# Loading tiles 0-1 from SyncE's DMA queue instead of ScalarE's, in a pruned matrix product

## The chip, the cores and the metric

The kernel runs on one core of one Trainium2 chip. The metric is the device time of one launch in microseconds (us); lower is better. Every number below comes from runs of the kernel before and from one profiled execution of it.

## The reference

The weights `w` (1024 x 1024, bf16) are pruned in groups of four along the rows: of each four values in a column, the two largest in magnitude stay and the others become zero. The pruned weights are then multiplied with the activations, and a bias is added.

```
B, S, D = 16, 512, 1024
wg   = w.reshape(D // 4, 4, D)
mag  = abs(wg)
thr  = second largest of mag along axis 1
wp   = (wg * (mag >= thr)).reshape(D, D)
out  = einsum("bsd,df->bsf", x, wp) + b
```

All is in bf16: 8192 tokens by 1024 inputs, 1024 outputs.

## The kernel before

The 8192 tokens are 64 tiles of 128. TensorE multiplies each tile with the pruned weights, eight blocks of 128 inputs and two halves of 512 outputs a tile; VectorE adds the bias as it moves the result out of PSUM; ScalarE's queue stores it. From tile 8 on a tile's transposed activations come from a transposing DMA (`xlead` for tiles 8 to 11, `xb` for the rest, 4 or 8 tiles at a time).

The first 30 us are different, because the weights must be pruned first. The weights are loaded in pieces, and each piece is pruned as it comes: magnitudes (`abs`), the larger and smaller of pairs (`hi`, `lo`), the threshold (`t1`, `t2`, `thr`), the mask and the product (`mask`, `mult`), nearly all on VectorE. Pieces 0 to 3 are 256 columns each of the upper half of the inputs, pieces 4 and 5 are 512 columns each of the lower half. In the first pieces a partition holds the four rows of one group; for later tiles the finished weights are spread to the natural order (`wp_nat`) by DMAs that SyncE (SP) issues, tokens `W0.0`, `W0.1` and so on.

Meanwhile TensorE works on tiles 0 to 7 with the pieces that are ready. Their activations are loaded by plain DMAs, `load_x`, and transposed on TensorE against an identity (line 189, token `T`); ScalarE copies the transposed tile from PSUM to SBUF (line 194, token `C`); then come the products of that tile with a piece (line 215, token `M7.0x` for tile 7, piece 0, first two of its four blocks). There are two PSUM banks for transposes, so a third transpose waits for the first copy. Before any of that TensorE runs products of constant ones into a bank that nobody reads (line 133), 22 in all, 8 of them under the token `F8`.

The order of each engine's work is written out by hand as a string of tokens, and `seq` chains the instructions of each engine in that order. TensorE starts `F8 T7a T5a T6a M7.0x M5.0x M6.0x T1a T0a M7.0y ...`; ScalarE starts `C7a C5a C6a C1a C0a`; SP's list is `W0.0 X0 X1 W0.1 Y1 ...`, where `X` and `Y` are transposing loads.

The loads at the very start are issued on two queues, SP's and ScalarE's (ACT's), by `issue(eng, ...)` at line 98: `load_w(g, c0, c1, ma, mb, eng)` loads rows `ma` to `mb` of the groups of half `g`, columns `c0` to `c1`; `load_x(ta, tb, eng)` loads the upper half of the inputs of tiles `ta` to `tb - 1`. In the order of lines 110 to 124 this makes, with the starts of the issues in the trace:

- SP: piece 0, row 0 (0.73) and row 2 (1.18); tiles 5-6 (1.64); piece 1 (2.11); tile 4 (2.99); tiles 2-3 (3.47); pieces 2 and 3 (3.95); piece 4 (4.55); the bias (5.23); piece 5 (6.10).
- ACT: piece 0, row 1 (0.74) and row 3 (1.17); tile 7 (1.66); tiles 0-1 (2.14); then the activation `spark` at line 116, whose table load starts at 2.63.

Of the kernel before, what the change touches and what calls it, by code (L numbers as in the profile page):

```python
# [10 lines left out]
def kernel(  # L11
# [64 lines left out]
    def act(i):  # L76
        return seq("act", i)
# [13 lines left out]
    def tokens(dram, t):  # L91
        a, b_ = next(s for s in GROUPS if s[0] <= t < s[1])
        return dram[a * P:b_ * P].rearrange("(p t) k -> p t k", p=P), t - a
    bias_sb = const.tile([P, Dout], bf16)

    def issue(eng, out_, in_):
        q = nc.sync if eng == "sp" else nc.scalar
        return seq(eng, q.dma_start(out_, in_))  # L98

    def load_w(g, c0, c1, ma=0, mb=4, eng="sp"):  # L100
        issue(eng, w_sb[:, g, ma:mb, c0:c1], wv[:, g, ma:mb, c0:c1])

    def load_x(ta, tb, eng="sp"):
        xs = const.tile([P, tb - ta, HK], bf16, name=f"x_{ta}")
        xv, n = tokens(xf, ta)
        issue(eng, xs[:], xv[:, n:n + tb - ta, :HK])
        for t in range(ta, tb):
            x_sb[t] = xs[:, t - ta, :]
# [3 lines left out]
    load_w(0, 0, 256, 2, 3)  # L112
    load_w(0, 0, 256, 3, 4, "act")
    load_x(7, 8, "act")
    load_x(0, 2, "act")
    act(nc.scalar.activation(spark[:], nc.const_aps.tensor(1.0, [P, 1], bf16), Act.Abs))
    load_x(5, 7)
    load_w(0, 256, 512)
    load_x(4, 5)
    load_x(2, 4)  # L120
# [368 lines left out]
```

## Time and profile before

| | |
|---|---|
| Median of 5 runs | 233.81 us (233.54 to 234.2) |
| The profiled execution's own time | 233.81 us |
| Its span, first to last instruction | 232.0 us |
| TensorE matmul (PE), busy | 226.7 us, 98% |
| VectorE (DVE), busy | 108.0 us, 47% |
| ScalarE (ACT), busy | 13.3 us, 6% |
| GpSimd (POOL), busy | 17.6 us, 8% |
| Granted TensorE clock | 1.0 throughout |

PE is the matmul side of TensorE and PEld its weight loads, which overlap the products. SPq and ACTq are the DMA issues of SyncE and ScalarE. A line such as `5.26 0.43 PE tp L189 x4` gives start and length in us, the engine, what it writes, the kernel's line and the number of instructions; `[0.44 <-DMA ...]` is idle time just before it and what ended it. In a table by stretches, each engine's busy time stands with its instruction count, then the granted clock, the share of the 16 DMA engines' time that was busy, and what they moved in GB/s.

### The profile page before, as it was taken

How to read it: one execution, taken by the hardware profiler on the slowest of the kernel's cores; microseconds unless marked ns; L12 is line 12 of the kernel's file. 1: busy time of each engine (PE TensorE's matmuls, PEld its weight loads, DVE VectorE, ACT ScalarE, POOL GpSimd, SP SyncE). 2: the span in 40 equal slices, each digit the busy share in tenths (PEclk: the TensorE clock that was granted, in tenths of full speed). 3: DMA queues.
4: the chain of work that ended last, by engine and by line, in shares of the span. 5: the costliest groups of instructions: out<-in, count | busy, mean ns of one | idle time of the engine just before them, and what ended most of it. 6: DMA issues, size and time to landing. Idle time of an engine off the chain costs nothing.

```text
span 232.0 us, 2828 instructions
## 1 busy us (share of the span) xinstructions
PE 226.7 (98%) x1139; PEld 112.2 (48%) x1158; DVE 108.0 (47%) x184; ACT 13.3 (6%) x27; POOL 17.6 (8%) x15
## 2 busy tenths in 40 slices
PE   7999999999999999999999999999999999999995
PEld 4787444544444444444444444444444444444443
DVE  4899867754234334334334324424424424423434
ACT  2665100000000000000000000000000000000000
POOL 1000199700000000000000000000000000000000
PEclk9999999999999999999999999999999999999999
DMA  6999999997299221992239821695228932122122
GB/s 186 354 215 216 222 182 252 345 206 271 95 217 280 90 93 50 233 278 75 90 96 262 230 93 48 165 285 147 84 90 197 271 120 76 62 90 82 58 89 90
DMA packets 78268, 38.19 MB, mean 165 GB/s; under 512 B 63664, under 2 KB 70576, under 8 KB 78256
## 3 DMA queue, kind: packets, MB, share of 16 engines
q1 hardware_dynamic: 67328, 20.61, 42.1%
q10 hardware_dynamic: 10928, 17.40, 20.8%
q8 instruction: 9, 0.15, 0.3%
q14 instruction: 3, 0.02, 0.1%
HBM read 3.41 MB, written 16.78 MB: 87 GB/s over the span
## 4 chain that ended last, share of the span: by engine, by line
PE 96%; DMA 2%; issue 1%; ACTq 0%; ACT 0%; DVE 0%
PE ps L238 87%; PE ps L215 6%; DMA x<-in_x_dram 2%; PE tp L238 1%; PE tp L189 1%; ACTq L98 0%; ACT xt L194 0%; DVE o L398 0%
## 5 line engine op out<-in xcount | busy, mean ns | idle before, releaser
L238 PE MATMUL ps<-wp_nat,xb 128*128 128x512 bf16 (+2 forms) x832 | 178.9, 375 | 0.8
L238 PEld LDWEIGHTS <-xb 128*128 128x128 bf16 x848 | 82.4, 98 | 97.5
L398 DVE TENSOR_TENSOR o<-ps,bias_sb 128x512 bf16<-128x512 f32 (+1 forms) x112 | 71.6, 677 | 114.3 <-PE ps L238 112.0
L394 POOL TENSOR_TENSOR st<-st,bias_sb 128x1024 f32<-128x1024 f32 x8 | 16.7, 2132 | 0.0
L215 PE MATMUL ps<-wp,xt 128*128 128x256 bf16 x128 | 15.1, 273 | 0.0
L238 PE MATMUL ps<-wp_nat,xlow 128*128 128x512 bf16 x62 | 14.0, 379 | 0.1
L215 PEld LDWEIGHTS <-xt 128*128 128x128 bf16 x128 | 12.2, 98 | 2.1 <-ACT xt L194 0.5
L400 DVE TENSOR_TENSOR o<-ps,st 128x512 bf16<-128x512 f32 x16 | 11.1, 692 | 2.8 <-PE ps L238 2.1
L238 PE MATMUL ps<-wp_nat,xlead 128*128 128x512 bf16 x47 | 11.1, 379 | 0.1
L238 PEld LDWEIGHTS <-xlow 128*128 128x128 bf16 x64 | 7.2, 112 | 6.7
L238 PEld LDWEIGHTS <-xlead 128*128 128x128 bf16 x64 | 6.2, 97 | 7.1
L255 ACT COPY st<-ps 128x512 f32<-128x512 f32 x16 | 8.5, 598 | 6.6 <-PE ps L215 4.3
L154 DVE TENSOR_TENSOR mag<-mag,hi 128x512 bf16<-128x512 bf16 (+2 forms) x8 | 5.4, 690 | 0.2
L154 DVE TENSOR_TENSOR wp<-w_sb,mag 128x512 bf16<-128x512 bf16 (+2 forms) x8 | 5.4, 690 | 0.2
L133 PE MATMUL ps<-const-bfloat16-1.0 128*128 128x128 bf16 (+1 forms) x22 | 3.9, 356 | 0.8 <-PEq L473 0.8
L164 DVE TENSOR_SCALAR mag<-w_sb 128x512 uint16<-128x512 uint16 (+2 forms) x6 | 2.7, 466 | 3.4 <-DMA w_sb<-in_w_dram 3.4
L238 PE MATMUL tp<-wp_nat,xlead 128*128 128x512 bf16 x16 | 4.1, 379 | 0.0
L189 PE MATMUL tp<-ident,x 128*128 128x128 bf16 x32 | 2.8, 220 | 0.8 <-DMA x<-in_x_dram 0.6
L133 PEld LDWEIGHTS <-const-bfloat16-1.0 128*128 128x128 bf16 x22 | 2.1, 125 | 2.4 <-issue 2.4
L154 DVE TENSOR_TENSOR hi<-mag 128x512 bf16<-128x512 bf16 (+2 forms) x7 | 3.2, 459 | 0.1
L154 DVE TENSOR_TENSOR lo<-mag 128x512 bf16<-128x512 bf16 (+2 forms) x7 | 3.2, 458 | 0.0
L194 ACT COPY xt<-tp 128x256 f32<-128x256 f32 x8 | 2.7, 380 | 3.6 <-PE tp L189 3.6
(15 smaller groups left out, 13.3 us busy)
## 6 DMA issues: line engine op xcount, KB each, us to landing
out_dram<-o ACTq DMA_DIRECT2D x59, 256.0 KB, 2.4
wp_nat<-wp SPq DMA_DIRECT2D x14, 128.0 KB, 3.5
w_sb<-in_w_dram SPq DMA_DIRECT2D x3, 512.0 KB, 6.9
out_dram<-o ACTq DMA_DIRECT2D x8, 128.0 KB, 1.7
x<-in_x_dram SPq DMA_DIRECT2D x2, 256.0 KB, 4.4
w_sb<-in_w_dram SPq DMA_DIRECT2D x1, 256.0 KB, 5.3
x<-in_x_dram ACTq DMA_DIRECT2D x1, 256.0 KB, 4.6
bias_sb<-in_b_dram SPq DMA_DIRECT2D x1, 256.0 KB, 6.9
```

The lines of the kernel that those rows point to most:

```text
L133: pe(nc.tensor.matmul(warm_ps[:, :rep * P], lhsT=nc.const_aps.tensor(1.0, [P, P], bf16), rhs=nc.const_aps.tensor(1.0, [P, rep * P], bf16), ...
L154: dve(nc.vector.tensor_tensor(out, a, b_, op=op))
L164: dve(nc.vector.tensor_single_scalar(self.mag[:, ms, :].bitcast(u16), self.w[:, ms, :].bitcast(u16), 0x7FFF, op=Alu.bitwise_and))
L189: pe(nc.tensor.transpose(tp[:, m, :], xg[:, m, :], ident[:]))
L194: act(nc.scalar.copy(xt[:].bitcast(fp32), xpk[t].bitcast(fp32)))
L215: pe(nc.tensor.matmul(ps[:, c0 + d:c1 + d], lhsT=xpk[t][:, m, :], rhs=wp[:, g, m, c0:c1], start=(new and m == ms.start), stop=(left[(q, n) ...
L238: pe(nc.tensor.matmul(ps, lhsT=xt[:, kt - koff, :], rhs=wp_nat[:, kt, c0:c1], start=(kt == first), stop=(kt == last)))
L255: act(nc.scalar.copy(st[:, n % 2, :, :].rearrange("p t c -> p (t c)"), ps_open.pop((q, n))[:]))
L394: pool(nc.gpsimd.tensor_tensor(st[:], st[:], bias[:, :, None, :].to_broadcast([P, 2, 2, CW]), op=Alu.add))
L398: dve(nc.vector.tensor_tensor(o[:, c0:c1], ps, bias_sb[:, c0:c1], op=Alu.add))
L400: dve(nc.vector.tensor_tensor(o[:, c0:c1].rearrange("p (n c) -> p n c", n=2), ps.rearrange("p (n c) -> p n c", n=2), add, op=Alu.add))
```

## The change

The load of tiles 0-1 is issued from SP's queue instead of ACT's. In the program it moves behind the load of tiles 5-6, so that on SP's queue it stands between tiles 5-6 and piece 1 of the weights. On ACT's queue the activation `spark` follows directly on the load of tile 7. Nothing else differs: the same bytes, the same tiles, the same order of work on TensorE, VectorE and ScalarE afterwards.

```
     load_w(0, 0, 256, 3, 4, "act")
     load_x(7, 8, "act")
-    load_x(0, 2, "act")
     act(nc.scalar.activation(spark[:], nc.const_aps.tensor(1.0, [P, 1], bf16), Act.Abs))
     load_x(5, 7)
+    load_x(0, 2)
     load_w(0, 256, 512)
     load_x(4, 5)
     load_x(2, 4)
```

More of the change, by code (lines that the diff above doesn't have):

```diff
@@ L114 @@
     load_x(7, 8, "act")
-    load_x(0, 2, "act")
     act(nc.scalar.activation(spark[:], nc.const_aps.tensor(1.0, [P, 1], bf16), Act.Abs))
     load_x(5, 7)
+    load_x(0, 2)
     load_w(0, 256, 512)
```

## The prediction, as put on record before the result

> **What bounds the kernel now.** I read first the page's chain, for the engine that sets the end; then the same chain in order of time, for the load on it; then the DMA issues of the first 2.5 us one by one; last the timelines, for the first user of each load that the change touches. The shares of the chain by engine:
>
> ```profile
> PE 96%; DMA 2%; issue 1%; ACTq 0%; ACT 0%; DVE 0%
> ```
>
> TensorE sets the end. A load can cost only if TensorE waits for what comes of it. The chain's start, columns start, length, what:
>
> ```profile
> 1.66 3.56 DMA x<-in_x_dram
> 5.21 0.05 issue
> 5.26 0.43 PE tp L189 x4
> 5.69 0.02 issue
> 5.71 0.38 ACT xt L194
> 6.09 0.04 issue
> 6.13 0.38 PE tp L189 x4
> ```
>
> The load on the chain is tile 7's, third on ACT's queue. It lands at 5.21; the last filler product ends at 4.70, so TensorE stands 0.56 us. Tile 6's transposes then wait for the copy of tile 7, because two banks are all that transposes have. Nothing after 6.13 in the chain is a load. So tile 7's landing goes into the end one for one, and every other load only past its slack. The loads issued between 1.6 and 2.3 us, from the DMA issues of that stretch (last number: us from issue to landing):
>
> ```profile
> x<-in_x_dram SPq DMA_DIRECT2D x1, 256.0 KB, 3.8
> w_sb<-in_w_dram SPq DMA_DIRECT2D x1, 256.0 KB, 5.3
> x<-in_x_dram ACTq DMA_DIRECT2D x1, 256.0 KB, 4.6
> x<-in_x_dram ACTq DMA_DIRECT2D x1, 128.0 KB, 3.6
> ```
>
> With the issues at 1.64, 2.11, 2.14 and 1.66 they land so: tiles 5-6 at 5.43, w's second piece (columns 256 to 511) at 7.41, tiles 0-1, the moved load, at 6.70, tile 7 at 5.21. Their users, from the timelines of PE, DVE and SP:
>
> ```profile
> 7.11 0.56 PEld L189 LDWEIGHTS <-x 128*128 128x128 bf16 x8
> 7.44 0.43 DVE L164 TENSOR_SCALAR mag<-w_sb 128x1024 uint16<-128x1024 uint16 x1 [0.44 <-DMA w_sb<-in_w_dram]
> 10.11 0.75 DVE L154 TENSOR_TENSOR wp<-w_sb,mag 128x512 bf16<-128x512 bf16 x2
> 10.89 2.56 SPq L98 DMA_DIRECT2D wp_nat<-wp  x4
> 13.49 4.62 SPq L223 DMA_TRANSPOSE xlead<-in_x_dram  x2
> 18.21 2.50 SPq L98 DMA_DIRECT2D wp_nat<-wp  x4
> ```
>
> Line one is the transposes of tiles 1 and 0, which use the moved load 0.41 us after it landed. Line two: VectorE stands 0.44 us for w's second piece and begins as it lands; this is the one place where the neighbour of the moved load is awaited. The other lines are what hangs on it: the pruning of that piece, the four spreads of finished weights that SP issues at its end, the two transposing loads behind them on SP, and the next four spreads.
>
> **The change part by part.** It takes one DMA issue of 256 KB off ACT's queue and puts it on SP's behind tiles 5-6 and ahead of w's second piece. No product, copy or byte is added. The profiled execution took 233.81 us, 232.0 of it span and 1.81 around it; the median of the five runs is the same 233.81, so the sum is made on 233.81.
>
> Removed: one ACT issue, 2.14 to 2.60 (0.47 us). The activation-table load behind it starts at about 2.14 instead of 2.63 and the spark activation ends 0.49 us earlier. ACT then stands 1.58 us until tile 7's transposes are done, so 0.00 us comes of it; the same idle time is the cover.
>
> Added: one SP issue. SP's next issue was due at 2.11, the old ACT issue at 2.14, so the moved load is issued 0.03 us earlier. Every SP issue behind it is later by the step between two such issues, 2.11 - 1.64 = 0.47 us: w's second piece (2.58), tile 4, tiles 2-3, w's other pieces. The bias load had started only at 5.23, after tile 7's landing at 5.21; now SP reaches it at about 5.65 and waits for nothing. The last load is issued by 7.25 instead of 6.77. SP's next work starts at 10.89, so 3.6 us of idle queue cover the issue itself: 0.00 us.
>
> Landings are the real question. The stretches 2:3 to 6:7 us by busy time (PE, PEld, DVE, ACT, POOL), then clock, DMA share and GB/s:
>
> ```profile
> 2.00:3.00 1.00, 1.00 (x4) 0.43 (x3) 0.00 (x1) 0.36 (x1) 0.00 (x0) 1.00 1.05 258
> 3.00:4.00 1.00, 1.00 (x9) 0.72 (x8) 0.97 (x5) 0.99 (x2) 0.00 (x0) 1.00 0.86 224
> 4.00:5.00 1.00, 0.70 (x12) 0.52 (x9) 0.93 (x6) 0.14 (x1) 0.00 (x0) 1.00 1.03 343
> 5.00:6.00 1.00, 0.64 (x8) 0.54 (x9) 0.93 (x3) 0.29 (x2) 0.00 (x0) 1.00 1.00 304
> 6.00:7.00 1.00, 0.83 (x9) 0.53 (x9) 0.96 (x3) 0.73 (x3) 0.00 (x0) 1.00 0.99 334
> ```
>
> The DMA engines are full from 2 us on. All that is due before w's second piece has landed is the same in both orders: 256 KB of w, 128 and 256 KB of tiles 7, 5, 6, 256 KB of tiles 0-1, 256 KB of the piece itself. With full engines and equal bytes the last byte comes at the same time, whichever queue asks. The issues run far ahead (w's second piece is asked for at 2.1 and lands at 7.4), so an issue 0.47 us later still finds a full backlog.
>
> Tile 7: still third on ACT's queue at 1.66, with nothing ahead of it changed; what goes was behind it. Bounds: -0.56 us if it lands at the fillers' end or earlier, +0.22 if it lands only with tiles 5-6 (5.43). I take 0.00, since its own row's issue and predecessors stay. Tiles 5-6, due at 5.51 after tile 7's transposes, lose the moved load as a neighbour on the other queue and gain none ahead: 0.00.
>
> Tiles 0-1: nearest rows are the old 4.6 us from issue and 4.8 and 5.0 of the later x loads on SP. From 2.11 that is 6.7 to 7.1, against 7.11 when they are needed: 0.00 us at both ends. I take 6.7.
>
> w's second piece: between 0.00 (equal bytes) and +0.47 (landing follows its issue) plus a whole moved load ahead of it. That load is 262 kB at the mean of 304 and 334 GB/s, 0.82 us; together +1.29. Nothing gains below zero, as TensorE waits nowhere for this piece. I take 0.00 because full engines are the nearest row. What delay is free I read from single instructions: the first product that needs the piece starts at 11.47, its weights are done at 10.52 (0.95 free); the first of the third piece starts at 14.96, weights done 14.17 (0.79); the last of the second four spreads lands at 23.73 and its product starts at 24.32 (0.59). The spread of 10.89 starts 0.03 us after the pruning ends and the SP queue runs without a gap up to the spread of 18.21, so a late piece comes through there one for one. The smallest slack is 0.59.
>
> Tile 4 (lands 7.79, used 8.86), tiles 2-3 (8.48, used 9.30) and w's third piece (9.96, used 10.78) have 1.07, 0.82 and 0.82 us, all above 0.47.
>
> Sum: 0.00 (ACT) + 0.00 (SP) + 0.00 (tile 7) + 0.00 (tiles 0-1) + 0.00 (piece two) = 233.8.
>
> A rule of the Trainium skill speaks against the change. Its page "DMA: Bandwidth & Descriptors", in the section "Queues, rings and completion order", says that each DMA engine takes turns between the queue rows that have work. By that, tiles 0-1 on ACT's row shared turns with w's second piece, and on SP's row they go wholly ahead of it; but both are done at the same total, so the rule makes the first bytes of the piece late and its last byte not. The same page, under "Issuing engines are not separate DMA queues", holds that a second issuing engine saves only issue time; by that the change costs the 0.47 us, which is covered. No trace here shows the two orders side by side.
>
> **The rivals.** *Slower: one queue alone feeds the engines worse.* The place is w's second piece. For it: from about 4.3 to 5.2 us most packets were ACT's, that is tiles 0-1, and w's second piece, asked for at 2.1, hardly moved before 5; if SP's queue can't be ready behind tiles 5-6, that time is lost. Against it: later SP alone moves 348 GB/s (7 to 8 us). Price: +1.29 on the piece, less 0.59 of slack, +0.70 us, 234.5; tiles 0-1, 0.82 later at 7.52 instead of 6.70, would stall 0.41 within that. It costs from the moment that VectorE starts on the piece later than 8.03, and over 0.2% (0.47 us, about what a measurement of this kernel can tell from no change) from 8.50.
>
> *Faster: tile 7 lands earlier.* For it: its sixteen parts land between 4.32 and 5.21, the last but one at 4.97, so one DMA engine lags, and with 256 KB less on ACT's queue that lag might go. Against: that load stood behind tile 7. At 4.97 it brings 0.24, 233.6, within 0.2%. Over 0.2% needs nearly the whole 0.56 (233.25), with tiles 5-6 early as well.
>
> *Nothing moves at all*, because the engines and not the queues set the order, is the forecast itself.
>
> **How the numbers follow.** Forecast 0.54, its own range 233.4 to 234.1 (0.24 early to 0.22 late on tile 7, and the runs' spread). Late second piece 0.33: the row between 4.3 and 5.2 us is real evidence. Tile 7 early by over 0.47 us 0.13. So faster 0.13, same 0.54, slower 0.33. The range runs from 233.2 (0.56 early) to 234.8 (0.70 late, with some 0.3 of the runs' spread).
>
> **What would show it.** Right: tile 7's transposes still start near 5.26, tiles 1 and 0 near 7.1 to 7.2 without a wait for a DMA, VectorE starts on piece two within 7.2 to 8.0, SP's spreads by 11.5, and TensorE waits for no spread at 24.3. Wrong: first transposes 0.3 us or more off 5.26; a DMA wait ahead of tile 1's transposes; VectorE's start on piece two after 8.5.

## The result, and the profile after

The changed kernel took 234.27 us (median; 233.77 to 234.88 in 22 executions) against 233.78 us before (233.4 to 234.2 in 42): 1.0021 times as long, 95% interval 1.0015 to 1.0027, or 0.49 us. It is a little slower; no change was forecast.

The profiled execution of the changed kernel was a lucky one: 233.86 us, span 232.1, against 233.81 and 232.0. It doesn't hold the loss, so it can only show what moved. Its chain, by engine, from the page:

```profile
PE 98%; issue 0%; DVE 0%
```

No load stands on this chain any more. Its start (start, length, what):

```profile
0.77 4.42 PE ps L133 x22
5.20 0.85 PE tp L189 x8
6.05 0.03 issue
6.08 0.50 PE tp L189 x4
```

Tile 7 landed before the fillers ended, so its transposes follow them without the 0.56 us gap. But they are slow: eight take 1.06 us (4.99 to 6.05), where before eight took 0.64. The granted clock came to full speed only at 6.36 us in this execution and at 3.98 in that of before; until then two transposes start 107 ns apart instead of 56. (These moments stand in the trace's own record of the clock; the clock column of the tables by stretches reads 1.00 already before them.) Both effects cancel: tile 1's transposes start at 7.27 instead of 7.21.

In what follows w's second piece is the load of piece 1, and w's third piece is the load of pieces 2 and 3 together. The first four spreads are `W0.0` and the second four `W0.1`. A hand-over is a place where TensorE takes up what a load, a spread or the pruning has made, and its room is the time by which that is ready before TensorE wants it.

The loads issued between 1.6 and 3.0 us, as in the prediction:

```profile
x<-in_x_dram SPq DMA_DIRECT2D x2, 256.0 KB, 3.5
w_sb<-in_w_dram SPq DMA_DIRECT2D x1, 256.0 KB, 4.6
x<-in_x_dram ACTq DMA_DIRECT2D x1, 128.0 KB, 3.1
```

Tiles 5-6 landed at 5.04, tiles 0-1 at 5.69 (1.0 earlier), tile 7 at 4.80, and w's second piece, issued at 2.64 instead of 2.11, at 7.21 (0.2 earlier). All that the prediction watched came in time. What came late is behind it. VectorE's and SP's timelines after the change:

```profile
7.23 0.43 DVE L164 TENSOR_SCALAR mag<-w_sb 128x1024 uint16<-128x1024 uint16 x1 [0.22 <-DMA w_sb<-in_w_dram]
9.90 0.75 DVE L154 TENSOR_TENSOR wp<-w_sb,mag 128x512 bf16<-128x512 bf16 x2
11.34 0.43 DVE L164 TENSOR_SCALAR mag<-w_sb 128x1024 uint16<-128x1024 uint16 x1 [0.69 <-DMA w_sb<-in_w_dram]
10.68 3.44 SPq L98 DMA_DIRECT2D wp_nat<-wp  x4
14.17 4.83 SPq L223 DMA_TRANSPOSE xlead<-in_x_dram  x2
19.10 2.50 SPq L98 DMA_DIRECT2D wp_nat<-wp  x4
```

Line three is new: VectorE stands 0.69 us for w's third piece, which landed at 11.32. Before it had landed at 9.96 and VectorE took it up at 10.78 without a wait. The first four spreads start 0.2 us earlier than before, but their issue takes 3.44 us instead of 2.56, and the second four start at 19.10 instead of 18.21. So SP's chain lost 0.9 us.

Fifteen of that load's sixteen parts had landed by 10.00 us (9.82 before); its last part lagged. The DMA engines also did less in the stretches from 5 us on (last two columns: DMA share and GB/s), first before:

```profile
5.00:5.75 0.75, 0.49 (x8) 0.49 (x9) 0.70 (x2) 0.04 (x1) 0.00 (x0) 1.00 0.98 294
7.00:8.00 1.00, 1.00 (x14) 0.95 (x15) 0.53 (x2) 0.36 (x2) 0.00 (x0) 1.00 1.01 348
```

then after:

```profile
5.00:5.75 0.75, 0.75 (x10) 0.75 (x9) 0.70 (x2) 0.09 (x1) 0.00 (x0) 1.00 0.72 212
7.00:8.00 1.00, 0.97 (x14) 0.92 (x14) 0.75 (x3) 0.30 (x2) 0.00 (x0) 1.00 0.94 321
8.00:9.00 1.00, 1.00 (x11) 0.90 (x10) 0.96 (x5) 0.34 (x2) 0.00 (x0) 1.00 1.00 302
```

From 5.00 to 5.75 us, and a little from 7 to 8, the DMA engines stood idle for part of the time, although loads of more than a megabyte had been issued and had not landed.

### The profile page after: what moved, and what is told of

Same layout as the page of the kernel before. It is cut to its first block, busy times and chain, and to the rows that moved or that the text cites. A ratio compares the mean times of both kernels' runs of the same rounds, so it can differ in the third digit from the quotient of the medians.

```text
span 232.1 us, 2828 instructions
## 1 busy us (share of the span) xinstructions
PE 227.6 (98%) x1139; PEld 113.1 (49%) x1158; DVE 108.0 (47%) x184; ACT 13.4 (6%) x27; POOL 17.6 (8%) x15
## 4 chain that ended last, share of the span: by engine, by line
PE 98%; issue 0%; DVE 0%
PE ps L238 87%; PE ps L215 6%; PE ps L133 2%; PE tp L238 1%; PE tp L189 1%; DVE o L398 0%
## 5 line engine op out<-in xcount | busy, mean ns | idle before, releaser
L133 PE MATMUL ps<-const-bfloat16-1.0 128*128 128x128 bf16 (+1 forms) x22 | 4.4, 396 | 0.8 <-PEq L473 0.8
L189 PE MATMUL tp<-ident,x 128*128 128x128 bf16 x32 | 3.3, 248 | 0.1
```

The costliest lines, as they stand in the source:

```text
L133: pe(nc.tensor.matmul(warm_ps[:, :rep * P], lhsT=nc.const_aps.tensor(1.0, [P, P], bf16), rhs=nc.const_aps.tensor(1.0, [P, rep * P], bf16), ...
L189: pe(nc.tensor.transpose(tp[:, m, :], xg[:, m, :], ident[:]))
```

## The experiments

Each set below ran on one chip with its own executions of the kernel before. A ratio is to those.

**The changed kernel again, three times.** No edit.

> The changed kernel once more. Two theories for its 0.49 us. 'Start': in most executions TensorE's transposes and first products begin later than before, because of the loads of x or the clock; the one profile of the changed kernel had them only 0.06 us late. 'Weights': pieces two and three of the weights and the spreads behind them come later and TensorE waits for them in most executions, though not in that profile. Both expect 234.2 to 234.4 again. In the profile the start theory expects tile 1's transposes (the fifth tile-wise step of TensorE) after 7.3 us and no stall later; the weights theory expects a stall of TensorE between 11 and 25 us.

> The changed kernel again, on the same chip as the next run. 0.1 to 0.5 us above before (1.0006 and 1.0021 in two sets of runs so far).

> The changed kernel on the same chip as the three others: 0.1 to 0.5 us above before.

Measured: 1.0006 (0.9997 to 1.0014), 1.0019 (1.0003 to 1.0035) and 1.0006 (0.9997 to 1.0015). The loss varies between sets. Over all 58 executions, the first 22 among them, it is 0.35 us on the mean above the median of before in the same set, give or take 0.11; 40% of them are more than 0.4 us above it, against 5% of 166 executions of before in the first five sets (7% of 189 with the sixth, which held four executions near 236 us). In the first set all executions but one lie above the median of before, and that one (233.77) lies at it. In the three repeats the fastest are as fast as before, and the loss is mostly a tail.

These profiles are lucky ones too (233.74, 233.96 and 233.67 us), but they show where time runs out. The stretch from 7 to 8 us (DMA share and GB/s last) in the second repeat:

```profile
7.00:8.00 1.00, 0.97 (x14) 0.90 (x14) 0.85 (x3) 0.29 (x3) 0.00 (x0) 1.00 0.75 207
```

and in the third:

```profile
7.00:8.00 1.00, 1.00 (x16) 0.94 (x14) 0.42 (x2) 0.59 (x2) 0.00 (x0) 1.00 0.75 229
```

In the first repeat the DMA share is 0.83. The first repeat has TensorE waiting 0.19 us at 24.25, and the last of the second four spreads landed at 24.20:

```profile
23.57 0.65 PE ps L238 x3
24.22 0.03 issue
24.25 1.24 PE ps L238 x5
```

The second waits 0.07 us at 24.48 (landed 24.44). The third has, among its waits after 8 us, one that before doesn't have:

```profile
PEld L189 <- DMA x<-in_x_dram: 0.2, 1, 0.2
```

That is tiles 2-3, landed at 9.24 when TensorE wanted them. So the start theory's late first transposes were not found in these profiles (6.91, 7.30 and 6.99 us for tile 1), and waits at two different hand-overs were. They are small. From the start of tile 1's transposes to the end of the span it takes 224.78 us in the profile of before (232.0 less 7.21), and 224.80, 225.05, 224.86 and 224.89 in the four of the changed kernel: 0.02 to 0.27 us of loss behind that start. The start itself differs more from profile to profile, 6.85 to 7.38 us over all the kernels below that keep the pruning, the two where tiles 0-1 came late left aside. Whether the executions with the loss, none of which was profiled, lose their time at the start or behind it is not shown.

**Without the pruning of pieces 1 to 5.** `do` returns without an instruction for every step but `mult` of these pieces, `mult` reads `w` twice, and `abs3` on ScalarE is empty; in both orders of loads.

> The kernel before without the magnitudes, thresholds and masks of pieces 1 to 5 of the weights (the weights are multiplied with themselves instead), so that finished weights and spreads are there microseconds early. It takes the weights' path out of the question. Both theories expect 233.6 to 233.9, since TensorE waits for no weights in the profile of before.

> The changed kernel with the same work left out (no magnitudes, thresholds and masks of pieces 1 to 5). Start theory: still 0.35 to 0.6 us above the same kernel with the old order of loads. Weights theory: within 0.15 us of it.

Measured: 239.37 and 237.46 us. The pair fails as a test. Two of the third four spreads (`W1.0q`) are issued by ScalarE, here later than before, and ScalarE copies two results out of PSUM only behind them. TensorE waited 3.3 and 2.1 us for the first of these copies (line 259 of this kernel), until 29.85 and 28.31 us. The chain without pruning, old order of loads:

```profile
28.61 0.56 ACTq L98
29.17 0.04 issue
29.21 0.59 ACT st L259
29.80 0.04 issue
29.85 1.86 PE ps L242 x4
```

There the granted clock then stood at 0.5 from 29.63 to 33.04 us, and four products took 1.86 us instead of 1.02 in the other. Nothing follows on the loads.

**The issue step alone.** Tiles 0-1 stay on ACT's queue.

```
     load_x(5, 7)
+    tiny = const.tile([P, 32], bf16)
+    issue("sp", tiny[:], xf[:P, :32])
     load_w(0, 256, 512)
```

> The kernel before, with one extra load of 8 KB on SP's queue in the place where the change puts tiles 0-1, so that every later issue on SP comes about 0.4 us later, while tiles 0-1 stay on ACT's queue. If the later issue of the weights is the cause (weights theory), 234.1 to 234.3. If the queue that carries tiles 0-1 is the cause (start theory, or one queue alone feeding worse), the same as before within 0.15 us.

Measured: 234.05 us, 1.0018 (1.0008 to 1.0029). DMA share from 7 to 8 us:

```profile
7.00:8.00 1.00, 1.00 (x16) 0.93 (x14) 0.79 (x3) 0.65 (x2) 0.00 (x0) 1.00 0.88 277
```

w's third piece landed at 11.04 and tiles 2-3 at 9.05, 0.04 us before TensorE wanted them. So the moved load is not needed for the loss: later issues on SP make it, with both queues carrying what they carried before. (They are 0.7 to 0.8 us later here, not 0.4, since the issue of w's second piece starts only at 2.94; so this is a larger dose than the change's.) The profiled execution, with these late landings and idle engines in it, took 233.54 us and was the fastest of its twelve. Late landings alone don't make the loss.

**The same step, further back.**

```
     load_x(2, 4)
+    tiny = const.tile([P, 32], bf16)
+    issue("sp", tiny[:], xf[:P, :32])
     load_w(0, 512, 1024)
```

> The kernel before with the extra load of 8 KB on SP's queue directly ahead of the third piece of the weights, so that tiles 5-6, the second piece, tile 4 and tiles 2-3 are issued as before and everything from the third piece on comes about 0.5 us later. If lateness from the third piece on is the cause: that piece lands at 10.6 us or later, its products start within 0.6 us of the finished weights, 0.15 to 0.4 us above before. If the loads ahead of it (tile 4, tiles 2-3) make the loss: the same as before within 0.1 us.

Measured: 233.9 us against 233.86 (0.9976, 0.9947 to 1.0006; the base of this set held four executions near 236 us, so the medians are the better comparison). And the expectation for the third piece was wrong:

```profile
7.00:8.00 1.00, 0.97 (x14) 0.89 (x14) 0.91 (x4) 0.29 (x2) 0.00 (x0) 1.00 1.11 336
```

Issued at 4.48, as late as in the changed kernel, it landed at 9.73. So in this profile its own issue time doesn't decide. What goes with the idle engines is ahead of it: in all seven profiles where tile 4 was issued by 3.1 us, here too, the DMA share from 7 to 8 us is 1.01 or more; in all eleven where it was issued after 3.3, it is 0.69 to 0.94 (the pair without pruning left aside). Tiles 2-3 are late together with tile 4 in these eleven, so the runs don't tell the two apart.

**SP's issues back in time.** Tiles 0-1 stay on SP's queue, and w's second piece goes to ACT's.

```
     load_x(7, 8, "act")
+    load_w(0, 256, 512, eng="act")
...
     load_x(0, 2)
-    load_w(0, 256, 512)
```

> The changed kernel with the second piece of the weights on ACT's queue behind tile 7, so that SP's later issues come 0.67 us earlier and both queues have work. If the later issues on SP leave the DMA engines short of work for some 0.3 us (as at 5.0 to 5.75 us in one profile and 7.0 to 7.5 us in the other), this closes that hole: no quarter microsecond under 60 KB between 4 and 8 us, 233.4 to 233.8. If one more load on SP doesn't matter, 233.85 to 234.3.

Measured: 233.94 us against 234.0, 1.0005 (0.9995 to 1.0015); the interval holds no change and also the small losses above. The profile is plain: 1.04 from 7 to 8 us, third piece at 9.88, second four spreads issued at 18.55.

**Tiles 0-1 behind w's second piece, both on SP.** The lines `load_x(0, 2)` and `load_w(0, 256, 512)` of the changed kernel change places.

> The changed kernel with tiles 0-1 on SP behind the second piece of the weights instead of ahead of it. The piece is then issued at 2.11 us as before, but all later loads on SP stay 0.47 us late and tiles 0-1 are asked for 0.67 us later. If the lateness of that one piece makes the loss, 233.6 to 233.85; if the later pieces and the hole do, 233.95 to 234.3; if tiles 0-1 come too late for TensorE (needed at about 6.9 us), a wait for a load ahead of their transposes.

Measured: 234.3 us, 1.0022 (1.001 to 1.0033). Tiles 0-1 landed at 8.43; the chain:

```profile
2.82 5.61 DMA x<-in_x_dram
8.43 0.05 issue
8.48 0.53 PE tp L189 x6
```

This profiled execution took 235.09 us. The third of the expected cases, then, with the hole as well (DMA share 0.93 from 7 to 8 us). TensorE stood 1.1 us for tiles 0-1 here, so the run doesn't tell whether the early issue of that piece alone would help.

**The hand-over of the second four spreads, relaxed.** `A2h1` are the first products of tile 10 with the second half of the outputs. They and the other tokens with `h1` read the second four spreads, those with `h0` the first four. Both kernels, in TensorE's order:

```
-  ... A0h0 A2h0 M7.3 A2h1 A1h0 A3h1 A0h1 A3h0 A1h1
+  ... A0h0 A2h0 M7.3 A1h0 A3h0 A2h1 A3h1 A0h1 A1h1
```

> The kernel before with the first products of tiles 8 to 11 in another order: both of the second half of the first four spreads (A1h0, A3h0) ahead of those that read the second four spreads (A2h1, A3h1), which gives the second four spreads 1.7 us more. Hand-over theory (TensorE waits in the changed kernel, in most executions, for the last of the second four spreads): 233.6 to 233.8, the same as before within 0.15 us, since TensorE had 0.59 us to spare there. Start theory: the same.

> The changed kernel with the same other order of the first products of tiles 8 to 11. Hand-over theory: the loss is gone, and what tile 7 gains by landing 0.4 us earlier (4.81 instead of 5.21 in two profiles) shows: 233.3 to 233.6, 0.1 to 0.4 us faster than before. Start theory (the loads of x make the loss): no change against the changed kernel, 233.85 to 234.3.

> The changed kernel with the hand-over relaxed by 1.7 us, again. Hand-over theory: 0.2 us or more below the changed kernel in the same call, and at or below before. If the loss sits elsewhere (start of TensorE, loads of x): the same as the changed kernel within 0.1 us.

Measured: before 0.9997 (0.9988 to 1.0006); changed 0.9995 (0.9987 to 1.0004), and in a second set 0.9998 (0.9989 to 1.0007), where the unrelaxed changed kernel had 1.0019. Over the 22 executions the relaxed changed kernel is 0.04 us below the median of before, give or take 0.11, against 0.35 above for the 58 unrelaxed ones. So no loss is seen once TensorE asks for these spreads later. But only the second set holds the unrelaxed changed kernel too, and there the medians are 233.95 relaxed and 234.05 unrelaxed; the means differ by more, 0.42 us, of which 0.16 come from one execution at 236.05. That is less than proof. And the profiles don't show what the theory needs, that the new order brings these spreads later: the last of them lands at 24.0 us on the mean in both orders (23.73, 24.20 and 24.18 in the three profiles of the old order with SP's own order of spreads, 23.58 to 24.44 in the seven of the new). With 24.20 the relaxed kernel before would have had no room either, had it kept the tight order: by an estimate from its start (7.10 against 7.21) it would have asked at 24.21.

**The same hand-over, tightened.** A2h1 directly behind A0h0, in both kernels.

> The kernel before with A2h1, the first user of the second four spreads, moved 1.3 us ahead (right behind A0h0), so that TensorE waits for the last of these spreads in every execution. It lands at 23.73 and 24.20 us in two profiles with the old order of loads; the wait would be about 0.7 us: 234.2 to 234.7. Alone it tells nothing; it is the base for the next run.

> The changed kernel with the same earlier A2h1. With TensorE waiting for the last of the second four spreads in every execution, the time is this landing plus a constant, so the difference to the run before is the mean delay of that landing over all executions. Hand-over theory: 0.2 to 0.5 us above it. If the change doesn't delay the spreads on the mean: within 0.1 us.

Measured: 1.0018 (1.0004 to 1.0032) and 1.0034 (1.0013 to 1.0055). TensorE waited 0.62 and 0.58 us in the profiles. The medians differ by 0.33 us, as the hand-over theory has it, but the intervals overlap, and the spread landed at 24.18 with the old order and 23.58 with the new in these two profiles. Inconclusive.

**The spreads themselves earlier.** SP's order `W0.0 X0 W0.1 X1` instead of `W0.0 X0 X1 W0.1`, in both kernels.

> The changed kernel with SP's second four spreads (W0.1) issued ahead of the second transposing load (X1) instead of behind it, so that they land 1 us or more earlier; TensorE's order is that of the changed kernel. Hand-over theory: the loss is gone, within 0.15 us of before or up to 0.3 us below it, and no wait of TensorE at 24.2 to 24.5 us in the profile. If the other order of the products had helped for another reason: still 0.2 us or more above before.

> The kernel before with the same order on SP's queue. Both theories: the same as before within 0.15 us, since TensorE has no wait for these spreads there in the profile.

Measured: 1.0006 (0.9998 to 1.0015) and 1.0001 (0.9991 to 1.001); the unrelaxed changed kernel had 1.0006 in this set. With the second four spreads landed by 22.53 TensorE has no wait at 24 us, but there was little loss in this set to take away. Inconclusive.

**The issue step alone, with the hand-over relaxed.** The first two edits together.

> The kernel before with the extra load of 8 KB on SP's queue (tiles 0-1 stay on ACT's), and with the hand-over relaxed by 1.7 us. With the tight hand-over the extra issue cost 0.3 us (1.0018). If the later issues cost at this hand-over, the loss is gone: 0 to 0.3 us below before. If elsewhere, still 0.2 us or more above.

Measured: 234.16 us, 1.0022 (1.0007 to 1.0036). The loss stays. So this hand-over is not the only place, at least with SP's issues 0.8 to 1.0 us late. Where the rest is lost is not shown: in this profile (233.92 us) tiles 2-3 and the third piece's products have 0.62 and 0.90 us of room, in that of the extra load alone 0.04 and 0.14.

**Both cures.** Second piece on ACT's queue and the hand-over relaxed.

> The changed kernel with the second piece of the weights on ACT's queue behind tile 7 (SP's later issues back in time, third piece at 9.9 us) and with the hand-over of the second four spreads relaxed by 1.7 us. Nothing late is left: 233.5 to 233.85, at or a little below before; what remains is TensorE's start.

Measured: 233.87 against 233.86 us, 0.9999 (0.9972 to 1.0026). Nothing is seen to beat the kernel before, but the interval is wide enough to hide a gain or a loss of half a microsecond.

## Why the prediction was wrong

Set side by side are four profiles with the old order of loads (before and its three reorderings) and eight with the new, the pair without pruning left aside.

- **Tile 7, taken at 0.00: right.** It lands at 4.88 to 5.21 (mean 4.99) in the old order and 4.80 to 5.38 (4.97) in the new. The 5.21 that I measured the stall by was the late end of a spread.
- **Tiles 0-1, taken at 6.7: too careful.** Mean 6.7 in the old order, 5.9 in the new, 6.43 at the latest. The tightened kernel of before waited 0.81 us for them in its profile (landed 7.71).
- **w's second piece, taken at 0.00: right in size.** Mean 7.34 in the old order, 7.47 in the new, with single late ones in both (8.24 and 8.23).
- **The loads behind it: the step that failed.** I let them come at most one issue step, 0.47 us, later, and found "1.07, 0.82 and 0.82 us, all above 0.47". The third piece comes 1.0 us later (mean 9.95 before, 10.99 after; 9.37 to 10.86 and 10.69 to 11.32). Not all of it: the eighth of its sixteen parts lands 0.25 us later (9.07 and 9.32), the fifteenth and the last a full microsecond. VectorE then takes it up as it lands in six of the eight, and the time from finished weights to their first product falls from 0.55 to 1.13 us to 0.05 to 0.73. Tiles 2-3 are down to 0.05 and 0.16 us in two of the eight. By the prediction's own figures 1.0 us would use up the 0.82 in front of VectorE and 0.2 of the 0.79 behind it, and still cost nothing on the mean. So this step explains how the room went, and only executions later than the mean can lose time by it.
- **Behind that the premise failed:** "an issue 0.47 us later still finds a full backlog". The DMA share from 7 to 8 us fell to 0.69 to 0.94, and equal bytes with idle engines land later. "Full from 2 us on" was a loose reading already before: the row from 3 to 4 us has 0.86.
- **The SP queue's cover of 3.6 us** was of the right size for the issues themselves. But the first four spreads and the transposing loads behind them take longer to issue, perhaps because the late weights are still landing then (the last of them at 14.83 us in the changed kernel's first profile, 13.69 before); that reason is not shown. In the seven new-order profiles with SP's own order the second four start at 18.83 to 19.32, in the three old ones at 18.21 to 19.24, 0.4 us earlier on the mean. That was counted nowhere. Their last landing, which is what TensorE waits for, is no later on the mean (24.0 in both).
- **The slower rival** had the right kind of cause, idle DMA engines, and the wrong place: it charged w's second piece, which was not late on the mean, and "one queue alone", where the extra 8 KB load shows that an issue step on SP is enough. Idle engines near 5 us, its place to look, show in the first profile of the changed kernel (0.72 from 5.00 to 5.75 us) and not in the three repeats (0.95 or more); 7 us was not foreseen.
- **The two rules of the Trainium skill**, from "DMA: Bandwidth & Descriptors": the one on turns between queue rows ("Queues, rings and completion order") charged the first bytes of the second piece; the profiles don't show its landing late on the mean. The one on issuing engines ("Issuing engines are not separate DMA queues"), that a second one saves only issue time, agrees with the extra 8 KB load, which costs about as much as the moved one (1.0018); but the prediction took that time as covered, and for the loads behind it it was not.

What is shown and what is not: shown are the idle DMA engines, the late third piece, the shrunk room at its products and at tiles 2-3, and that later issues on SP alone bring a loss of the same size. That no loss is seen with the second four spreads' hand-over relaxed speaks for that place, but the landing there is not later on the mean. Not shown is one execution of the changed kernel with the full loss in a profile; the waits caught there are 0.07 to 0.19 us, not 0.5. So how the late loads become the lost time stays open, TensorE's start is not ruled out for the executions that have it, and the extra load with the hand-over relaxed, where the loss stays, speaks for more than one place. Why engines run dry at 7 us when tile 4 is issued after 3.3 us, with loads outstanding, and don't when only the third piece is late, is open too.

## What to carry to other kernels

Moving a DMA issue from one queue to another moves every later issue on the second queue by one issue step; follow all of them to their users, not only the neighbour, and ask for more room than the step itself: here the third piece came twice the step later. The median of a kernel with several hand-overs of 0.6 to 1 us of room depends on the tail of its loads: one profile with nothing late says little, and a set of eight shows more. A second queue that looks idle may be what keeps the first one's issues early: here its one load, moved, put every later issue on SP back by 0.4 to 0.6 us.

## What the runs showed of the hardware that was not expected

- The moment of full clock differs from execution to execution with the same first 4 us of products: from 3.49 to 6.36 us in the profiles above.
- The last of a load's sixteen parts can lag: w's third piece in the changed kernel's first profile had fifteen parts by 10.00 us and the last at 11.32. It happens in the old order too (9.74 and 10.86 in the tightened kernel before).
- The DMA engines' share fell to 0.69 for a microsecond while more than half a megabyte of issued loads had not landed (the relaxed changed kernel, 7 to 8 us).
